# Attention scores of a unit issued as one run of products over five accumulator banks, instead of three runs

## The chip, the cores and the metric

The kernel runs on one core of a Trainium2 chip. The metric is the device time of one execution in microseconds (us). Below, TensorE is the matrix engine (PE in the profile, its weight loads PEld), VectorE is DVE, ScalarE is ACT, GpSimd is POOL, and SyncE (SP) issues the DMAs.

## The reference

Windowed attention with a linear distance bias on 8 batches of 8 heads, then a two-layer MLP with GELU on the attention's output:

```
batch, n_heads, seq, head_dim = 8, 8, 576, 64        # window 128
scores = q @ k.T / sqrt(64)
scores = where(0 <= i - j < 128, scores - slope[h] * |i - j|, -1e9)
attn = exp(scores - max); attn = attn / (sum(attn) + 1e-9)
x = (attn @ v) as (8 * 576, 512)
out = gelu(x @ w_in) @ w_out                          # 512 -> 2048 -> 512
```

The inputs are float32. The kernel splits each operand into a high and a low float16 part and adds three products (high by high, low by high, high by low); only the first batch's attention and the first token tile's second layer run on float32 operands.

## The kernel before, in words

**Units.** Attention works in units of one batch `b` and one pair of heads `hp`, so 4 units to a batch, 32 in all. A query block of 64 rows sees a window of 192 keys. The 18 blocks of a unit (9 blocks, 2 heads) are held two and two on the 128 partitions, as 9 groups of 128 x 192 scores (`GROUPS`, L43). Groups are put into PSUM in five banks of two or one groups: `BANKS = ((0, 1), (2, 3), (4,), (5, 6), (7, 8))`. Banks (0,1) and (5,6) belong to head 0, banks (2,3) and (7,8) to head 1, and bank (4,) holds block 8 of both heads. The first three banks are called EVEN, the last two ODD.

**Scores.** `scores(st, banks)` takes the PSUM banks of a piece, issues its products (L394), has VectorE bring each bank to SBUF as `s`, scaled and with the bias added (L416), and GpSimd write the masked corner (L421). Every product is a 64 x 64 weight (a query block) with 192 keys streaming. The head sets which half of the array's rows it uses, the half of the group which half of its columns. In a piece of two banks four products in a row use the four quarters of the array; in the piece of bank (4,) two in a row do. A unit has three pieces (`PIECES`): banks (0,1) and (2,3) with 24 products, bank (4,) with 6, banks (5,6) and (7,8) with 24.

**Softmax and weighing.** `softmax` does EVEN and then ODD: VectorE takes the row maximum (L480), ScalarE the exponentials with their sums (L483, 5 and 4 of them, given to the planner with a raised priority), VectorE the reciprocals (L486, L487), GpSimd the high half of the weights (`e_main`, L489), VectorE the low half (L491, under the helper's line L143), and one transposing DMA on the SP queue writes `et` (L492). `weigh` multiplies `et` with v (`av`, L529) in two PSUM banks, one for each of the token tiles that a batch's rows fall into (`b` and `b + 1`, since a batch has 576 rows and a tile 512). ScalarE (L542) and VectorE (L543, shown as L143) bring each `av` into the MLP's input `x` of that tile. `x` has two buffers.

**The MLP.** Tokens go in 9 tiles `t` of 512. A tile has 32 steps. In steps 0 to 15 `mlp_in` makes one block of the hidden layer with 12 products of 128 x 512 (`h`, L573), ScalarE applies Gelu (L589), GpSimd and VectorE split it into the halves `g` (L590, L591 shown as L143). In steps 16 to 31 `mlp_out` adds 12 products to an output bank `o` (L611), four steps to a bank.

**Banks.** PSUM has 8 banks, in two tags of 4: "att" for scores (from batch 1 on) and for `av`, "mm" for `h` and `o`.

**Order.** Into tile `t`'s 32 steps the work of batch `b = t + 1` is set by hand (L720 to L757). For `t >= 2`, `SCORES_AT = (2, 11, 16, 21)` and `WEIGH_AT = (12, 20, 25, 30)`: the three pieces of unit 0 follow steps 2, 3 and 4, and after the third comes its softmax; unit 0 is weighed after step 12; and so on. Step 1 splits v and issues the loads of the next batch, step 6 takes the next v's maximum, step 24 splits the next q and k. The program text is the order of priority, and a planner (`TileContext` with `schedule_with_timeline_sim=True`) turns it into a fixed order of instructions on each engine: where an instruction's operand or buffer isn't free by the planner's own reckoning, a later one that is ready goes ahead of it. On the chip, each engine then keeps to that order and waits on semaphores.

The order by hand, in the lines that matter:

```
for t in range(1, NTILE):
    b = t + 1
    ...
    for step in range(2 * NFC):
        ...mlp_in(t, step) or 12 products of mlp_out...
        if step in at:
            hp, i = at[step]
            scores(unit(b, hp), BANKS[PIECES[i]])
            if i == 2:
                softmax(unit(b, hp))
        ...
        if step in weigh_at:
            weigh(unit(b, weigh_at.index(step)))
```

Of the kernel before, what the change touches and what calls it, by code (L numbers as in the profile page):

```python
# [11 lines left out]
F32 = mybir.dt.float32  # L12
I32 = mybir.dt.int32
AF = mybir.ActivationFunctionType
ALU = mybir.AluOpType
AX = mybir.AxisListType

B, H, S, D = 8, 8, 576, 64
WINDOW = 128
P = 128  # L20
QB = 64
# [8 lines left out]
W = 3 * QB  # L30
PAD = W - QB
NKB = 5
NEG = -1.0e30
# [3 lines left out]
EXACT = 1  # L37
# [5 lines left out]
GROUPS = [(h, j) for h in range(2) for j in (0, 4)] + [(None, 8)] + [(h, j) for h in range(2) for j in (1, 5)]  # L43
NG = len(GROUPS)
NEVEN = 5
FIRST_MM = (2,)
EXP_AHEAD = 400
BANKS = ((0, 1), (2, 3), (4,), (5, 6), (7, 8))
PIECES = (slice(0, 2), slice(2, 3), slice(3, 5))


@with_exitstack
def attention_gelu_mlp(
# [10 lines left out]
    nc = tc.nc  # L64
    pool = ctx.enter_context(tc.tile_pool(name="sb", bufs=1))
    psum = ctx.enter_context(tc.tile_pool(name="ps", bufs=1, space=bass.MemoryType.PSUM))

    def small(shape, name, bufs, tag=None, dt=F32):
        return pool.tile(shape, dt, tag=tag or name, name=name, bufs=bufs)
# [8 lines left out]
    ident, upper, never = (adders[:, n] for n in range(3))  # L78
# [206 lines left out]
    qbuf = pool.tile([P, 2, NPAIR * S], F16, name="qbuf")  # L285
    kbuf = pool.tile([P, 2, KS], F16, name="kbuf")
    qbuf32 = qbuf.rearrange("p h s -> p (h s)").bitcast(F32)
    kbuf32 = kbuf.rearrange("p h s -> p (h s)").bitcast(F32)
# [4 lines left out]
    v32s, qk32, csq = {}, {}, {}  # L293

    def load_v(b):
        v32 = pool.tile([P, NPAIR, NKB, P], F32, tag="v32", name=f"v32_{b}", bufs=1)
        for hp in range(NPAIR):
            nc.sync.dma_start(v32[:, hp], vp[b, hp].rearrange("(n p) d -> p n d", p=P))
        v32s[b] = v32
# [18 lines left out]
    def split_v(b):  # L318
        v32 = v32s.pop(b).rearrange("p h n d -> p (h n d)")
        hi = vbuf[:, 0].rearrange("p h n d -> p (h n d)")  # L320
        lo = vbuf[:, 1].rearrange("p h n d -> p (h n d)")
        nc.scalar.activation(hi, v32, AF.Copy, scale=scv[b])  # L322
        low_part(lo, v32, scv[b], hi)
# [38 lines left out]
    def bias_of(hp, head):  # L362
        return bias_p[:, hp : hp + 1, :] if head is None else bias_h[:, 2 * hp + head : 2 * hp + head + 1, :]

    def scores(st, banks):

        b, hp, u = st.b, st.hp, st.u
        if not hasattr(st, "s"):
            st.ps = {}
            st.s = pool.tile([P, NG, W], F32, tag="s", name=f"s{u}", bufs=2)  # L370
        s = st.s
        exact = b < EXACT
        terms = (None,) if exact else ((0, 0), (1, 0), (0, 1))

        def operands(term, r, j):
            q, k = slice(hp * S + j * QB, hp * S + (j + 1) * QB), slice(hp * S + PAD + (j - 2) * QB, hp * S + PAD + (j + 1) * QB)
            if exact:
                return qbuf32[r, q], kbuf32[r, k]
            return qbuf[r, term[0], q], kbuf[r, term[1], k]

        ps = st.ps
        for bank in banks:
            tag = "mm" if b == 0 and bank[0] in FIRST_MM else "att"
            ps[bank] = psum.tile([P, 2, 256], F32, tag=tag, name=f"sc{u}_{bank[0]}", bufs=4)
        for n in range(len(banks[0])):
            for i, term in enumerate(terms):
                for half in range(2):
                    for bank in banks:
                        head, j = GROUPS[bank[n]]
                        h = half if head is None else head  # L390
                        jj = j if head is None else j + 2 * half
                        r, o = slice(h * D, h * D + D), slice(half * D, half * D + D)
                        a, m = operands(term, r, jj)
                        nc.tensor.matmul(  # L394
                            ps[bank][o, n, 0:W], a, m, start=(i == 0), stop=(i == len(terms) - 1 and b > 0),
                            skip_group_check=True,
                        )
            if b == 0:
                for bank in banks:
                    adds = [(slice(0, W), ident, bias_of(hp, GROUPS[bank[n]][0])[:, 0])]  # L400
                    gap = (2 - GROUPS[bank[n]][1]) * QB
                    if gap > 0:

                        adds.append((slice(0, gap), upper, never[:, 0:gap]))
                    for i, (c, a, m) in enumerate(adds):
                        nc.tensor.matmul(
                            ps[bank][:, n, c], a, m, start=False, stop=(i == len(adds) - 1), skip_group_check=True
                        )
        if b == 0:
            return  # L410
        cs = csq[b]
        for bank in banks:
            head, k = GROUPS[bank[0]][0], len(bank)
            j = GROUPS[bank[0]][1]
            bias = bias_of(hp, head)
            nc.vector.scalar_tensor_tensor(  # L416
                out=s[:, bank[0] : bank[0] + k, :], in0=ps[bank][:, 0:k, 0:W], scalar=cs,
                in1=bias.broadcast_to([P, k, W]) if k > 1 else bias, op0=ALU.mult, op1=ALU.add,
            )
            if j < 2:  # L420
                nc.gpsimd.memset(s[0:D, bank[0], 0 : (2 - j) * QB], NEG)  # L421

    EVEN, ODD = slice(0, NEVEN), slice(NEVEN, NG)

# [124 lines left out]
    def tile_scales(t, ns):  # L549


        k = len(ns)
        r = slice(ns[0], ns[-1] + 1)
        big = k > 1
        gs = small([P, k], f"gs{t}_{ns[0]}", 2, tag=f"gs{int(big)}")
        nc.vector.tensor_scalar(gs, pww[:, r], pwx[t], 2.0 ** -26, op0=ALU.mult, op1=ALU.mult)
        if t == 0:
            for n in ns:
                gsc[t, n] = gs[:, n - ns[0] : n - ns[0] + 1]
            return  # L560
        sg = small([P, k], f"sg{t}_{ns[0]}", 2, tag=f"sg{int(big)}")
        nc.vector.tensor_scalar(sg, sww[:, r], sx[t], 2.0 ** -22, op0=ALU.mult, op1=ALU.mult)
        for n in ns:
            gsc[t, n], gsg[t, n] = gs[:, n - ns[0] : n - ns[0] + 1], sg[:, n - ns[0] : n - ns[0] + 1]
# [30 lines left out]
    def out_scale(t):  # L595
        so[t] = small([P, 1], f"so{t}", 2, tag="so")
        nc.vector.tensor_scalar(so[t], pwm, pwx[t], 2.0 ** -17, op0=ALU.mult, op1=ALU.mult)
# [29 lines left out]
    def unit(b, hp):  # L627
        if (b, hp) not in units:
            units[b, hp] = Unit(b, hp)
        return units[b, hp]  # L630

    def all_scores(st):
        for piece in PIECES:
            scores(st, BANKS[piece])

    fetched = iter(range(2 * NWP))

# [16 lines left out]
    fetch(NWP)  # L654

    all_scores(unit(0, 0))
    softmax_first(unit(0, 0))
    all_scores(unit(0, 1))
# [43 lines left out]
    scores_at, weigh_at, split_at = {1: 2, 3: 3}, {2: 0, 4: 1, 6: 2}, {5: 0, 6: 2, 7: 4}  # L702
# [18 lines left out]
    for t in range(1, NTILE):  # L721
        b = t + 1
        scores_at, weigh_at = (SCORES_AT, WEIGH_AT) if t > 1 else ((8, 14, 18, 22), (17, 22, 26, 30))
        at = {s + i: (hp, i) for hp, s in enumerate(scores_at) for i in range(3)}
        tile_scales(t, range(NWP))
        out_scale(t)
        for step in range(2 * NFC):
            if step < NFC:
                mlp_in(t, step)
            else:  # L730
                tb, q = divmod(step - NFC, 4)
                for fc in range(4 * q, 4 * q + 4):
                    mlp_out(t, tb, fc)
            if b >= B:
                continue
            if step in at:
                hp, i = at[step]
                scores(unit(b, hp), BANKS[PIECES[i]])
                if i == 2:
                    softmax(unit(b, hp))  # L740
            if step == 1:
                split_v(b)
                if b + 1 < B:
                    load_v(b + 1)
                    load_qk(b + 1)
            if step == 6:
                if b + 1 < B:
                    stat_v(b + 1)
                else:

                    pwx[B], sx[B] = pwv[B - 1], scv[B - 1]
                    cx_last = small([P, 1], "cxl", 1)
                    nc.vector.tensor_scalar(cx_last, pwv[B - 1], sx[B], 2.0 ** -27, op0=ALU.mult, op1=ALU.mult)
            if step in weigh_at:
                weigh(unit(b, weigh_at.index(step)))
            if step == SCORES_AT[-1] + 3 and b + 1 < B:
                split_qk(b + 1)  # L757
# [36 lines left out]
```

## Time and profile before

| What | Value |
|---|---|
| Median of 3 runs | 963.53 us (963.16 to 969.68) |
| The profiled execution's own time | 963.32 us |
| Its span, first to last instruction | 961.4 us |
| TensorE busy | 922.8 us, 96% |
| VectorE busy | 643.7 us, 67% |
| ScalarE busy | 436.6 us, 45% |
| GpSimd busy | 255.8 us, 27% |

The profile is of one execution. A row of the timeline gives the start, the length, the engine, the line, and how many instructions of one kind it holds; the length of a row of products goes to the modelled end of the last one, so the time that a run takes is read from its start to the start of the next row. A value in square brackets at the end of a row is idle time of the engine ahead of it and what ended it. A row of the waits tells who waited for whom: us in total, times, longest. Tile 2 begins at 297 us, tile 7 at 792 us; tiles 2 to 6 are those in which batches 3 to 7 are worked on.

### The profile page before, as it was taken

Reading aid. Unit: us, or ns where it says so; the run is one execution under the profiler, and the core shown is the slowest. Engines: PE = TensorE matmul, PEld = TensorE weight load, DVE = VectorE, ACT = ScalarE, POOL = GpSimd, SP = SyncE. Lnnn points to the kernel's source line nnn. Section 1 sums busy time; section 2 is a strip of 40 time slices with the busy share of each in tenths; the row PEclk is TensorE's granted clock in tenths of the full one; section 3 lists DMA queues with packets and bytes.
Section 4 is the critical chain, followed back from the end, with each engine's and each line's share of the span. In section 5 each row is a group of like instructions: output and inputs, shape, how many; then the busy total and the mean of one; then the engine's idle time right before and its main releaser. Section 6 shows DMA issues by size and latency. Waiting matters only on the chain. (4 is left out here: it accounts for less than half of the span.)

```text
span 961.4 us, 17491 instructions
## 1 busy us (share of the span) xinstructions
PE 922.8 (96%) x6996; PEld 446.1 (46%) x6996; DVE 643.7 (67%) x1270; ACT 436.6 (45%) x943; POOL 255.8 (27%) x516
## 2 busy tenths in 40 slices
PE   7988999769999899999999999999999999999998
PEld 3553444334454345444544444444544454444443
DVE  6699999989985877688767876777566632201300
ACT  6565445545553565256526653564465413201200
POOL 1010103324441433144313530363144312201200
PEclk9789999989999999999999999999999999999999
DMA  9525742972466224713372357244313430000000
GB/s 320 201 69 167 235 137 39 217 201 60 84 130 157 50 50 80 206 40 61 85 194 49 59 94 171 56 78 83 79 25 57 83 73 12 1 22 23 1 12 33
DMA packets 172451, 91.18 MB, mean 95 GB/s; under 512 B 132561, under 2 KB 153169, under 8 KB 172241
## 3 DMA queue, kind: packets, MB, share of 16 engines
q1 hardware_dynamic: 172368, 90.06, 37.9%
q8 instruction: 55, 0.90, 0.4%
q14 instruction: 28, 0.22, 0.1%
HBM read 46.53 MB, written 9.44 MB: 58 GB/s over the span
## 5 line engine op out<-in xcount | busy, mean ns | idle before, releaser
L573 PE MATMUL h<-x,wi 128*128 128x512 f16 x1728 | 386.7, 382 | 9.6 <-ACT g L589 3.9
L573 PEld LDWEIGHTS <-wi 128*128 128x128 f16 x1728 | 166.6, 98 | 212.4 <-issue 14.0
L611 PE MATMUL o<-wo,g 128*128 128x512 f16 x1152 | 259.9, 379 | 0.0
L611 PEld LDWEIGHTS <-g 128*128 128x128 f16 x1536 | 145.9, 98 | 174.3
L590 POOL TENSOR_SCALAR g<-g,sg 128x512 f16<-128x512 f32 x128 | 100.1, 786 | 288.7 <-ACT g L589 281.7
L143 DVE SCALAR_TENSOR_TENSOR g<-g,sg,g 128x512 f16<-128x512 f32 x128 | 106.2, 843 | 92.0 <-POOL g L590 92.0
L483 ACT ACTIVATE s<-s,nmax 128x192 f32<-128x192 f32 x252 | 111.2, 443 | 107.7 <-DVE nmax L480 105.0
L489 POOL TENSOR_SCALAR e_main<-s,z 128x192 f16<-128x192 f32 x252 | 124.3, 511 | 114.9 <-issue 37.3
L589 ACT ACTIVATE g<-h,gs 128x512 f32<-128x512 f32 x128 | 85.9, 687 | 137.3 <-PE h L573 108.5
L143 DVE SCALAR_TENSOR_TENSOR e_main<-s,z,e_main 128x192 f16<-128x192 f32 x252 | 112.1, 487 | 11.1 <-POOL e_main L489 10.8
L611 PE MATMUL o<-wo_first,g 128*128 128x512 f16 x384 | 88.2, 379 | 0.0
L394 PE MATMUL sc<-kbuf,qbuf 64*64 64x192 f16 (+1 forms) x1656 | 77.6, 266 | 9.4 <-DMA kbuf<-kp 4.4
L416 DVE SCALAR_TENSOR_TENSOR s<-sc,cs,bias_h 128x384 f32<-128x384 f32 x112 | 63.9, 606 | 15.1 <-PE sc L394 14.9
L542 ACT ACTIVATE x<-av,cx 128x448 f16<-128x448 f32 (+6 forms) x52 | 23.9, 477 | 86.0 <-PE av L529 85.8
L480 DVE TENSOR_REDUCE nmax<-s 128x5 f32<-128x960 f32 (+1 forms) x56 | 58.5, 1044 | 2.2
L608 PE MATMUL o<-zo,g 128*128 128x512 f32 x128 | 57.0, 598 | 0.0
L529 PE MATMUL av<-et,vbuf 128*64 128x128 f16 (+1 forms) x1680 | 45.2, 213 | 11.4 <-DMA et<-e_main 10.3
L421 POOL MEMSET s<- 64x128 f32 (+1 forms) x112 | 19.6, 176 | 134.5 <-DVE s L416 133.7
L619 ACT ACTIVATE ob<-o,so 128x512 f32<-128x512 f32 x16 | 10.9, 679 | 96.9 <-PE o L611 96.8
L394 PEld LDWEIGHTS <-qbuf 64*64 64x64 f16 x1512 | 35.2, 106 | 42.0 <-issue 39.4
L529 PEld LDWEIGHTS <-vbuf 128*64 128x64 f16 x1680 | 42.2, 113 | 21.3 <-issue 19.5
L621 DVE TENSOR_SCALAR ob<-o,so 128x512 f32<-128x512 f32 x16 | 11.9, 744 | 60.0 <-PE o L611 60.0
(128 smaller groups left out, 715.1 us busy)
## 6 DMA issues: line engine op xcount, KB each, us to landing
v<-vp SPq DMA_DIRECT2D x32, 320.0 KB, 5.0
out<-ob SPq DMA_DIRECT2D x36, 256.0 KB, 2.1
raw<-w_in SPq DMA_DIRECT2D x8, 1024.0 KB, 14.1
raw<-w_out SPq DMA_DIRECT2D x8, 1024.0 KB, 5.0
q<-qp SPq DMA_DIRECT2D x7, 1152.0 KB, 6.1
k<-kp SPq DMA_DIRECT2D x7, 1152.0 KB, 6.3
qbuf<-qp SPq DMA_DIRECT2D x4, 288.0 KB, 4.5
kbuf<-kp SPq DMA_DIRECT2D x4, 288.0 KB, 4.9
```

The lines of the kernel that those rows point to most:

```text
L143: nc.vector.scalar_tensor_tensor(out=dst, in0=src, scalar=scale, in1=high, op0=ALU.mult, op1=ALU.subtract)
L394: nc.tensor.matmul(ps[bank][o, n, 0:W], a, m, start=(i == 0), stop=(i == len(terms) - 1 and b > 0), skip_group_check=True,)
L416: nc.vector.scalar_tensor_tensor(out=s[:, bank[0] : bank[0] + k, :], in0=ps[bank][:, 0:k, 0:W], scalar=cs, in1=bias.broadcast_to([P, k, W] ...
L480: nc.vector.tensor_reduce(out=nmax[:, r], in_=s[:, r], axis=AX.X, op=ALU.max, negate=True)
L483: nc.scalar.activation(s[:, i, :], s[:, i, :], AF.Exp, bias=nmax[:, i : i + 1], accum_out=z[:, i : i + 1])
L489: nc.gpsimd.tensor_scalar(e[:, i, 0, c], s[:, i], z[:, i : i + 1], 1.0, op0=ALU.mult, op1=ALU.mult)
L529: nc.tensor.matmul(av[r, (j - blocks[0]) * QB : (j - blocks[0] + len(js)) * QB], v32s[b][:, hp, kb, r] if b < EXACT else vbuf[:, vi, hp, k ...
L573: nc.tensor.matmul(ph, wi[n][:, a, cc, k * P : (k + 1) * P], x[:, cc, b, :], start=(i == 0), stop=(i == 3 * NCC - 1),)
L589: nc.scalar.activation(g32, ph, AF.Gelu, scale=gsc[t, n])
L590: nc.gpsimd.tensor_scalar(g[:, r, 0], g32, gsg[t, n], 1.0, op0=ALU.mult, op1=ALU.mult)
L608: nc.tensor.matmul(o, g[:, r, c], zo[n][:, n % 2, k * DM : (k + 1) * DM], start=(fc == 0), stop=(fc == NFC - 1))
L611: nc.tensor.matmul(o, g[:, r, a, c], wo[n][:, b, k, :], start=(fc == 0 and i == 0), stop=(fc == NFC - 1 and i == 2),)
```

## The change

From tile 2 on, that is for batches 3 to 7 (20 units), a unit's scores are no longer three pieces after three steps. All 54 products are issued together after the third of these steps (4, 13, 18, 23), in the order banks (0,1) and (2,3), banks (5,6) and (7,8), bank (4,); then come the five copies to `s`, in the order of the banks, and the softmax. Five banks are taken at once: four of tag "att" and, for bank (4,), one of tag "mm". The units of batches 1 and 2 keep their three pieces, those of batch 0 have a function of their own, `scores_first`, with the same instructions as before.

```diff
+TOGETHER = (BANKS[0:2], BANKS[3:5], BANKS[2:3])
...
-    def scores(st, banks):
+    def scores(st, pieces):
...
+        for bank in sum(pieces, ()):
+
+            tag = "mm" if len(bank) == 1 and len(pieces) > 1 else "att"
+            ps[bank] = psum.tile([P, 2, 256], F32, tag=tag, name=f"sc{u}_{bank[0]}", bufs=4)
+        terms = ((0, 0), (1, 0), (0, 1))
+        for banks in pieces:
+            for n in range(len(banks[0])):
+                for i, (a, m) in enumerate(terms):
+                    for half in range(2):
+                        for bank in banks:
...
+                            nc.tensor.matmul(
+                                ps[bank][o, n, 0:W], qbuf[r, a, q : q + QB], kbuf[r, m, k : k + W],
+                                start=(i == 0), stop=(i == len(terms) - 1), skip_group_check=True,
+                            )
+        for bank in sorted(ps):
...
+            nc.vector.scalar_tensor_tensor(
+                out=s[:, bank[0] : bank[0] + k, :], in0=ps[bank][:, 0:k, 0:W], scalar=csq[b],
...
     def all_scores(st):
         for piece in PIECES:
-            scores(st, BANKS[piece])
+            if st.b < EXACT:
+                scores_first(st, BANKS[piece])
+            else:
+                scores(st, (BANKS[piece],))
...
-        at = {s + i: (hp, i) for hp, s in enumerate(scores_at) for i in range(3)}
+        whole = t >= 2
+        at = {s + i: (hp, i) for hp, s in enumerate(scores_at) for i in ((2,) if whole else range(3))}
...
-                scores(unit(b, hp), BANKS[PIECES[i]])
+                scores(unit(b, hp), TOGETHER if whole else (BANKS[PIECES[i]],))
```

More of the change, by code (lines that the diff above doesn't have):

```diff
@@ L363, in bias_of, with scores_first @@
         return bias_p[:, hp : hp + 1, :] if head is None else bias_h[:, 2 * hp + head : 2 * hp + head + 1, :]
-    def scores(st, banks):
+    def scores(st, pieces):
+        b, hp, u = st.b, st.hp, st.u
+        if not hasattr(st, "s"):
+            st.s = pool.tile([P, NG, W], F32, tag="s", name=f"s{u}", bufs=2)
+        s = st.s
+        ps = {}
+        for bank in sum(pieces, ()):
[7 more added lines that the diff above has]
+                        for bank in banks:
+                            head, j = GROUPS[bank[n]]
+                            h, j = (half, j) if head is None else (head, j + 2 * half)
+                            r, o = slice(h * D, h * D + D), slice(half * D, half * D + D)
+                            q = hp * S + j * QB
+                            k = q + PAD - 2 * QB
+                            nc.tensor.matmul(
[3 more added lines that the diff above has]
+        for bank in sorted(ps):
+            head, j = GROUPS[bank[0]]
+            k = len(bank)
+            near = bias_of(hp, head)
+            nc.vector.scalar_tensor_tensor(
+                out=s[:, bank[0] : bank[0] + k, :], in0=ps[bank][:, 0:k, 0:W], scalar=csq[b],
+                in1=near.broadcast_to([P, k, W]) if k > 1 else near, op0=ALU.mult, op1=ALU.add,
+            )
+            if j < 2:
+                nc.gpsimd.memset(s[0:D, bank[0], 0 : (2 - j) * QB], NEG)
+    def scores_first(st, banks):
         b, hp, u = st.b, st.hp, st.u
@@ L370, in scores, with operands @@
             st.s = pool.tile([P, NG, W], F32, tag="s", name=f"s{u}", bufs=2)
[L371 to L375, printed above, removed]
+        def operands(r, j):
             q, k = slice(hp * S + j * QB, hp * S + (j + 1) * QB), slice(hp * S + PAD + (j - 2) * QB, hp * S + PAD + (j + 1) * QB)
-            if exact:
-                return qbuf32[r, q], kbuf32[r, k]
-            return qbuf[r, term[0], q], kbuf[r, term[1], k]
+            return qbuf32[r, q], kbuf32[r, k]
@@ L381, in scores @@
         ps = st.ps
         for bank in banks:
-            tag = "mm" if b == 0 and bank[0] in FIRST_MM else "att"
+            tag = "mm" if bank[0] in FIRST_MM else "att"
             ps[bank] = psum.tile([P, 2, 256], F32, tag=tag, name=f"sc{u}_{bank[0]}", bufs=4)
         for n in range(len(banks[0])):
[L386 to L397, printed above, removed]
@@ L398, in scores @@
-            if b == 0:
-                for bank in banks:
[L400 to L421, printed above, removed]
+            for half in range(2):
+                for bank in banks:
+                    head, j = GROUPS[bank[n]]
+                    h = half if head is None else head
+                    jj = j if head is None else j + 2 * half
+                    r, o = slice(h * D, h * D + D), slice(half * D, half * D + D)
+                    a, m = operands(r, jj)
+                    nc.tensor.matmul(ps[bank][o, n, 0:W], a, m, start=True, stop=False, skip_group_check=True)
@@ new lines, in scores_first @@
+            for bank in banks:
+                adds = [(slice(0, W), ident, bias_of(hp, GROUPS[bank[n]][0])[:, 0])]
+                gap = (2 - GROUPS[bank[n]][1]) * QB
+                if gap > 0:
+                    adds.append((slice(0, gap), upper, never[:, 0:gap]))
+                for i, (c, a, m) in enumerate(adds):
+                    nc.tensor.matmul(
+                        ps[bank][:, n, c], a, m, start=False, stop=(i == len(adds) - 1), skip_group_check=True
+                    )
```

## The prediction

> **What bounds the kernel now.** I read the page's busy shares first, then the busy times by tile, then TensorE's timeline through a tile, and last the waits.
>
> ```profile
> span 961.4 us, 17491 instructions
> ...
> PE 922.8 (96%) x6996; PEld 446.1 (46%) x6996; DVE 643.7 (67%) x1270; ACT 436.6 (45%) x943; POOL 255.8 (27%) x516
> ```
>
> ```profile
> core 0: us, PE busy (x) PEld busy (x) DVE busy (x) ACT busy (x) POOL busy (x), PEclk, DMA share, GB/s
> 297.00:399.00 102.00, 98.86 (x912) 47.90 (x910) 74.30 (x152) 51.33 (x112) 32.71 (x68) 0.98 0.41 94
> 399.00:497.00 98.00, 97.93 (x821) 47.41 (x820) 74.94 (x151) 51.63 (x112) 32.56 (x68) 1.00 0.43 98
> 497.00:596.00 99.00, 96.68 (x863) 46.72 (x862) 74.03 (x150) 50.99 (x112) 32.30 (x68) 1.00 0.45 97
> 596.00:695.00 99.00, 97.82 (x820) 47.20 (x819) 70.33 (x150) 53.73 (x113) 33.38 (x68) 1.00 0.34 73
> 695.00:792.00 97.00, 97.00 (x842) 46.97 (x841) 57.56 (x111) 45.50 (x109) 32.65 (x68) 1.00 0.34 61
> ```
>
> These are tiles 2 to 6, the only ones the change touches. TensorE is busy in all but 0 to 3 us of each, at nearly full granted clock; VectorE, the next busiest, has a quarter of the tile free. So time is gained here only by shorter work on TensorE, and lost by new waits of TensorE.
>
> The timeline of TensorE in tile 4 shows what the scores cost it:
>
> ```profile
> 531.41 2.76 PE L573 MATMUL h<-x,wi 128*128 128x512 f16 x12
> 534.11 0.43 PE L394 MATMUL sc<-kbuf,qbuf 64*64 64x192 f16 x6
> 534.47 1.60 PE L529 MATMUL av<-et,vbuf 128*64 128x128 f16 x66
> 536.00 2.76 PE L573 MATMUL h<-x,wi 128*128 128x512 f16 x12
> ...
> 544.50 2.75 PE L611 MATMUL o<-wo_first,g 128*128 128x512 f16 x12
> 547.19 0.69 PE L394 MATMUL sc<-kbuf,qbuf 64*64 64x192 f16 x24
> 547.81 2.76 PE L611 MATMUL o<-wo,g 128*128 128x512 f16 x12
> 550.50 0.43 PE L394 MATMUL sc<-kbuf,qbuf 64*64 64x192 f16 x6
> 550.87 2.76 PE L611 MATMUL o<-wo,g 128*128 128x512 f16 x12
> 553.56 0.69 PE L394 MATMUL sc<-kbuf,qbuf 64*64 64x192 f16 x24
> 554.18 2.76 PE L611 MATMUL o<-wo,g 128*128 128x512 f16 x12
> 556.78 2.75 PE L611 MATMUL o<-wo_first,g 128*128 128x512 f16 x12
> 559.47 1.60 PE L529 MATMUL av<-et,vbuf 128*64 128x128 f16 x66
> 561.00 2.76 PE L611 MATMUL o<-wo,g 128*128 128x512 f16 x12
> ```
>
> Two groups of 12 with nothing between them start 556.78 - 554.18 = 2.60 us apart. What stands between two groups costs their distance less 2.60. A piece of 24 products: 547.81 - 544.50 - 2.60 = 0.71 us. The piece of 6: 550.87 - 547.81 - 2.60 = 0.46. An `av` run alone: 561.00 - 556.78 - 2.60 = 1.62. The 6 together with `av` (step 12 of unit 1): 536.00 - 531.41 - 2.60 = 1.99, so there the 6 add only 0.37, because the change of shape into and out of small products is paid once for both.
>
> **What a longer run costs.** Four products in a row use four quarters of the array, so 24 are 6 rounds; the 6 of bank (4,) go two and two, 3 rounds. From 0.71 and 0.46, three rounds cost 0.25, a round 0.083, and the fixed part is 0.21 us a run. The whole unit is 6 + 6 + 3 = 15 rounds: 0.21 + 15 x 0.083 = 1.46 us. The trace has one such run, in the first tile, where the planner put several pieces together:
>
> ```profile
> 144.41 1.43 PE L394 MATMUL sc<-kbuf,qbuf 64*64 64x192 f16 x42
> 145.77 3.70 PE L608 MATMUL o<-zo,g 128*128 128x512 f32 x8
> ```
>
> Its 42 products take 1.36 us to the next start; beside it, the 24 take 547.81 - 547.19 = 0.62. If the cost went by the number of products (0.25 us for 18), the 42 would take 0.87. By rounds, 15 of them take 0.62 + 9 x 0.083 = 1.37. Rounds it is, and a run of three pieces isn't stretched by its length.
>
> [...]
>
> **The change part by part.**
>
> *Three runs become one, units 0, 2 and 3.* Before: 0.71 + 0.46 + 0.71 = 1.88. After: 1.46. Gain 0.42 us a unit, all of it on TensorE's path.
>
> *Unit 1.* Its 6 shared their entry with `av`, so before it cost 0.71 + 0.37 + 0.71 = 1.79; in one run it would gain 0.33. But the run needs all four "att" banks, and at step 13 one of them isn't free. `weigh` of unit 0, just ahead at step 12, fills two, and the second belongs to tile t + 2, whose `x` buffer is still being read by `mlp_in` of tile t up to step 15 (544.50):
>
> ```profile
> 535.06 0.42 ACT L542 ACTIVATE x<-av,cx 128x192 f16<-128x192 f32 x1 [0.16 <-PE av L529]
> ...
> 542.88 1.28 ACT L483 ACT_TABLE_LOAD   x1
> 545.81 0.45 ACT L483 ACTIVATE s<-s,nmax 128x192 f32<-128x192 f32 x1 [1.64 <-DVE nmax L480]
> ...
> 547.57 0.56 ACT L542 ACTIVATE x<-av,cx 128x384 f16<-128x384 f32 x1
> ```
>
> ```profile
> 529.67 4.27 DVE L143 SCALAR_TENSOR_TENSOR g<-g,sg,g 128x512 f16<-128x512 f32 x4
> 533.86 1.13 DVE L416 SCALAR_TENSOR_TENSOR s<-sc,cs,bias_h 128x384 f32<-128x384 f32 x2
> ...
> 535.57 0.41 DVE L416 SCALAR_TENSOR_TENSOR s<-sc,cs,bias_p 128x192 f32<-128x192 f32 x1
> ...
> 542.11 1.13 DVE L416 SCALAR_TENSOR_TENSOR s<-sc,cs,bias_h 128x384 f32<-128x384 f32 x2
> ...
> 548.17 0.62 DVE L143 SCALAR_TENSOR_TENSOR x<-av,cx,x 128x384 f16<-128x384 f32 x1
> ```
>
> The first `av` bank leaves at once, the second at 548.79, 12 us later. Before, three free banks were enough for any piece. After, bank (7,8) must wait, and the planner will let what is ready go ahead: 24 + 12 + 6 products at step 13 (the 12 on one head are two in a round, so 15 rounds, 1.46 us), the other 12 after step 15 or 16 (6 rounds, 0.71). Unit 1 then costs 2.17 instead of 1.79, a loss of 0.38. Its bounds are the gain of 0.33 (if the planner finds four banks free) and, from above, the late second half in the rivals. I take the loss, because the read of `x` up to step 15 lies in the program and not in anyone's speed.
>
> *The five copies to `s`.* 2 x 1.13 + 0.41 = 2.67 us of VectorE at a stretch, where they came in three parts. They delay the rows behind them on VectorE (`g`, the maximum of v at step 6) by up to 2 us. Cover: `g` of the first half isn't read before step 16, and the next taker of "att" banks is two or more steps (5.2 us) away, but for unit 1. Counted 0; if the cover goes, see the third rival.
>
> *The "mm" bank.* At worst VectorE starts 2.5 us late (531.41 to 533.86, behind four `g` rows) and reaches bank (4,) in its place, so the bank is back some 5 us after the run, two groups of `h`; three banks hold three groups. Counted 0.
>
> *Softmax later.* EVEN's scores come two steps later, but EVEN waited for bank (4,) anyway, and ODD's chain ends last. With both maxima ready together, ScalarE can do nine exponentials in one block (9 x 0.45) instead of two blocks with a Gelu between. That ends unit 0's chain earlier; I count nothing for it in the sum.
>
> *Waits that are there now.* By tile, TensorE's waits in tiles 2 to 6, and last one from before them:
>
> ```profile
> PE h L573 <- ACT g L589: 2.7, 2, 2.4
> PE av L529 <- DMA et<-e_main: 0.5, 1, 0.5
> ```
>
> ```profile
> PE av L529 <- DMA et<-e_main: 1.7, 1, 1.7
> PE h L573 <- ACT g L589: 0.6, 1, 0.6
> ```
>
> ```profile
> PE av L529 <- DVE g L143: 1.2, 1, 1.2
> ```
>
> ```profile
> PE sc L394 <- DVE s L416: 3.4, 1, 3.4
> ```
>
> The first five add up to 6.7 us (tiles 2, 4 and 5). They lie on the softmax chain and on Gelu, which the change rearranges: between all of it gone (-6.7) and as much again (+6.7). I take 0. The last is a scores run that stood waiting for the copy of an earlier one: it is what a too tight hold on the banks costs.
>
> **Sum.** A tile: 3 x 0.42 - 0.38 = 0.88 us; five tiles: 4.4. Against the profiled execution's 963.32 us (span 961.4 and 1.9 around it; the median is 963.53), that is **958.9 us**.
>
> **Rivals.**
>
> *Nothing breaks.* Unit 1 finds its banks and all 20 runs are whole: 15 x 0.42 + 5 x 0.33 = 7.95, so 955.4. For it: the planner may weigh unit 0 after unit 1's scores. Against it: `weigh` is ahead in the program. If the waits of 6.7 us shrink by half or more as well, both cases reach 955 to 950. Nine exponentials in one block speak for this.
>
> *Unit 1's second half comes too late (slower).* Before, its last copy ends at 543.24 (542.11 + 1.13), and its last transposing DMA lands as these rows tell:
>
> ```profile
> 543.96 9.79 SPq L492 DMA_TRANSPOSE et<-e_main  x2
> ```
>
> ```profile
> DMA to landing us min/median/max: 4.6/4.6/4.6
> ```
>
> The second was issued in 551 to 552, so it lands at about 556.3, and `av` starts at 559.47: 3.1 us to spare. After, if the bank leaves at 548.79 as now, 12 products (0.71) and a copy (0.57) end at 550.1, 6.8 us later than before; 3.7 us of wait a tile, 18.5 in five: 977.4. It decides from 0.9 us of wait a tile on. Against the full price: the bank's copy at 547.57 stands behind four exponentials of ODD that will no longer be ahead of it, and a planner that sees `et` late puts `av` one group (2.60) further back; then some 1 us is left, and 964.
>
> *Evacuation becomes the bound.* [...] In rows: the run takes 1.46 and its copies 2.67; with VectorE behind and ScalarE in its 6.6 us block (9 x 0.45 and two table loads of 1.28), the ten units of the first half could each hold an `h` by 1 us: 958.9 + 10 = 969. Against it: one such wait of 2.4 is the longest now, with shorter blocks but more table loads.
>
> *The change doesn't do what it says.* The planner cuts most runs as in tile 0, and entries stay as many as before: 963.
>
> **Chances.** Forecast 0.45; nothing breaks or the waits shrink 0.27; second half too late 0.15 (a third of it near the full price); evacuation 0.05; no real change 0.08. The range that leaves out 2 in 10 runs from 950 to 970. A measurement of this kernel tells about 1% (9.6 us) from no change. Faster by more, below 953.9, needs whole runs and shrunken waits together: 0.13. Slower by more, above 973, needs the late half near its full price: 0.09. Within: 0.78.
>
> **What would show it.** Right: in tiles 2 to 6 the rows of L394 lose their x24, x6, x24 pattern; units 0, 2, 3 show one row of 54 with about 1.46 between the groups around it; unit 1 shows 42 and then 12 after step 15, with the 12 right behind the copy of `x`. Wrong: a row of 54 for unit 1, or 54 taking more than 1.6 us; waits of `av` on `et` at step 20 of every tile; waits of `h` on Gelu after steps 4 and 13; clock below 0.98 in these tiles. The forecast falls if waits of TensorE in tiles 2 to 6 sum to over 12 us or under 2.

## The result and the profile after

| | Before | After |
|---|---|---|
| Median, us (20 runs each) | 962.78 (953.61 to 969.68) | 971.39 (963.53 to 977.84) |
| Ratio, 95% interval | | 1.0102 [1.0075, 1.0129] |
| Profiled execution, us (span) | 963.32 (961.4) | 971.82 (970.0) |

The kernel became 1.0% slower; 958.9 had been predicted. Ratios leave out runs over 1.5% above the fastest of their kernel (mean granted clock 0.960 to 0.975 where it is on record, 0.966 to 0.995 in those kept), so a ratio can rest on fewer runs than the median beside it. The page of the changed kernel, its head:

```profile
span 970.0 us, 17465 instructions
...
PE 923.4 (95%) x6996; PEld 455.0 (47%) x6996; DVE 646.4 (67%) x1270; ACT 412.0 (42%) x925; POOL 258.1 (27%) x516
```

TensorE has the same 6996 products. ScalarE has 18 instructions and 24.6 us less: it loads its tables 42 times in place of 60 (18 x 1.28 = 23.0 us), since nine exponentials now mostly stand in one block. By tile, in the columns of the prediction's second fence:

```profile
398.00:499.00 101.00, 97.95 (x830) 48.65 (x828) 74.71 (x150) 45.88 (x107) 33.56 (x68) 0.98 0.40 93
499.00:600.00 101.00, 97.92 (x856) 49.44 (x854) 74.53 (x150) 46.09 (x108) 33.24 (x68) 0.98 0.42 96
600.00:703.00 103.00, 99.44 (x884) 50.18 (x882) 70.05 (x150) 47.76 (x109) 33.78 (x68) 0.98 0.35 75
```

Tiles 3 to 5 (97.3, 99.5 and 98.3 us long before, from the first `h` of one to that of the next) are 101.0, 100.6 and 103.0 us long, at a granted clock of 0.98 in place of 1.00. TensorE's timeline shows where, here the whole of tile 4 up to unit 2 and the same place of the other four tiles (in square brackets is the idle time ahead of the row, and what ended it):

```profile
337.64 2.77 PE L544 MATMUL av<-et,vbuf 128*64 128x128 f16 x66 [2.75 <-DMA et<-e_main]
...
438.42 1.81 PE L544 MATMUL av<-et,vbuf 128*64 128x128 f16 x54 [2.73 <-DMA et<-e_main]
440.16 4.13 PE L588 MATMUL h<-x,wi 128*128 128x512 f16 x12
...
499.06 1.67 PE L588 MATMUL h<-x,wi 128*128 128x512 f16 x7
500.89 1.55 PE L544 MATMUL av<-et,vbuf 128*64 128x128 f16 x54 [0.16 <-DMA et<-e_main]
...
513.92 1.43 PE L388 MATMUL sc<-kbuf,qbuf 64*64 64x192 f16 x54
515.29 21.17 PE L588 MATMUL h<-x,wi 128*128 128x512 f16 x96
539.25 2.77 PE L544 MATMUL av<-et,vbuf 128*64 128x128 f16 x66 [2.80 <-DMA et<-e_main]
541.96 2.76 PE L588 MATMUL h<-x,wi 128*128 128x512 f16 x12
544.65 1.42 PE L388 MATMUL sc<-kbuf,qbuf 64*64 64x192 f16 x42
546.00 3.41 PE L588 MATMUL h<-x,wi 128*128 128x512 f16 x15
549.35 0.68 PE L388 MATMUL sc<-kbuf,qbuf 64*64 64x192 f16 x12
549.96 2.12 PE L588 MATMUL h<-x,wi 128*128 128x512 f16 x9
...
554.50 5.34 PE L626 MATMUL o<-wo,g 128*128 128x512 f16 x24
559.78 1.43 PE L388 MATMUL sc<-kbuf,qbuf 64*64 64x192 f16 x54
561.14 2.76 PE L626 MATMUL o<-wo,g 128*128 128x512 f16 x12
...
640.25 2.20 PE L544 MATMUL av<-et,vbuf 128*64 128x128 f16 x54 [2.77 <-DMA et<-e_main]
...
739.44 1.57 PE L544 MATMUL av<-et,vbuf 128*64 128x64 f16 x60 [1.48 <-DMA et<-e_main]
```

The scores cost what was forecast: a whole run 561.14 - 554.50 - 2 x 2.60 = 1.44 us, unit 1's 42 products 546.00 - 541.96 - 2.60 = 1.44. What is new is the wait at step 12: the `av` run of **unit 0** waits for its `et` in every tile, 2.75, 2.73, 2.80, 2.77 and 1.48 us. From the end of each of the four long waits, give or take 1.1 us, the granted clock is 0.50 for 3.4 us (which waits had this with them is in the last section). The windows around the wait in tile 4:

```profile
538.00:540.00 2.00, 0.75 (x22) 0.75 (x24) 0.70 (x1) 0.00 (x0) 0.16 (x1) 0.63 0.34 63
540.00:542.00 2.00, 2.00 (x53) 1.94 (x50) 1.08 (x2) 0.42 (x1) 0.00 (x0) 0.51 0.00 0
```

The clock column, the last but two, reads 0.51 from 540 to 542. The `av` run then takes 541.96 - 539.25 = 2.71 us, 1.18 more than the 1.53 of before (536.00 - 534.47); in tile 3 the 12 `h` behind it take 4.13 in place of 2.76.

**The account.** From the first `h` of tile 2 to the first of tile 7, before took 495.9 us and after 502.9: 7.0 of the 8.5 us between the two profiled executions. The other 1.5 lie ahead of tile 2, where both issue the same products, in the same order but for two neighbours. Between the starts of two successive products there is a usual distance for each kind of pair (two of 128 x 512: 2.60 / 12 = 0.217 us); what goes beyond it by over 0.3 us adds up to 7.2 us in these tiles before and 14.5 after. With the scores' gain worked out by the same distances (4.5 us), a rest of 7.0 + 4.5 - 7.3 = 4.2 us is left. I put it down to the half clock, in four places where before had one. A second trace bears this out: the kernel with the maximum of v at step 9 (below) waits 13.0 us where the change waits 14.0, its profiled execution has a mean granted clock of 0.980 where the change's has 0.976, and its tiles 2 to 6 are 497.4 us long, 5.6 less.

**Why unit 0's `et` is late.** VectorE in tile 4 of after, from the maximum of v on:

```profile
514.14 2.82 DVE L209 TENSOR_REDUCE stv<-v 128x1 f32<-128x2560 f32 x1 [1.90 <-DMA v<-vp]
...
517.60 1.12 DVE L396 SCALAR_TENSOR_TENSOR s<-sc,cs,bias_h 128x384 f32<-128x384 f32 x2
...
520.00 1.14 DVE L396 SCALAR_TENSOR_TENSOR s<-sc,cs,bias_h 128x384 f32<-128x384 f32 x2
521.06 0.41 DVE L396 SCALAR_TENSOR_TENSOR s<-sc,cs,bias_p 128x192 f32<-128x192 f32 x1
521.45 1.99 DVE L495 TENSOR_REDUCE nmax<-s 128x4 f32<-128x768 f32 x2
...
531.74 2.58 DVE L144 SCALAR_TENSOR_TENSOR e_main<-s,z,e_main 128x192 f16<-128x192 f32 x5
```

and the same work in tile 4 of before:

```profile
505.52 1.14 DVE L416 SCALAR_TENSOR_TENSOR s<-sc,cs,bias_h 128x384 f32<-128x384 f32 x2 [0.49 <-PE sc L394]
508.22 2.82 DVE L208 TENSOR_REDUCE stv<-v 128x1 f32<-128x2560 f32 x1 [1.56 <-DMA v<-vp]
...
511.62 0.41 DVE L416 SCALAR_TENSOR_TENSOR s<-sc,cs,bias_p 128x192 f32<-128x192 f32 x1
...
527.77 1.78 DVE L143 SCALAR_TENSOR_TENSOR e_main<-s,z,e_main 128x192 f16<-128x192 f32 x3
```

Before, EVEN's two big copies were over before v's maximum came, and EVEN's five exponentials were done before ODD's four began. After, the maximum of v is taken right as the run of 54 starts, so the run's first copy comes 3.7 us behind that start (517.60 - 513.92), and bank (4,), which EVEN needs, is copied last of the five. GpSimd in after:

```profile
525.55 2.27 POOL L504 TENSOR_SCALAR e_main<-s,z 128x192 f16<-128x192 f32 x4 [3.53 <-issue]
...
530.00 3.35 POOL L504 TENSOR_SCALAR e_main<-s,z 128x192 f16<-128x192 f32 x5
```

The four groups of ODD go through first, EVEN's five last. VectorE's last row ends at 534.32, 35.26 us into a tile that starts at 499.06; before, its last ended at 529.55, 32.63 us into a tile that starts at 496.92. The transposing DMA of the last half follows, here before (issued at 529.58, four groups) and after (issued at 534.34, five groups):

```profile
DMA to landing us min/median/max: 4.2/4.2/4.2
DMA to landing us min/median/max: 4.9/4.9/4.9
```

To the hundredth, it lands 4.27 us behind VectorE before (533.82) and 4.89 in after (539.21). `av` stood at 37.55 us into the tile before (534.47), so the chain had 37.55 - 32.63 - 4.27 = 0.65 us to spare; in tile 3 it had 0.41 and in tile 5 0.13. In after, `av`'s place is at 37.40 (536.46, where the eight groups of `h` end). So the chain is 2.63 later, its DMA 0.62 longer and the place 0.15 earlier: less the 0.65, this is 2.75 us. The row has 2.80; `av` starts 0.04 us behind the landing.

### The profile page after: what moved, and what is told of

It reads as the page before. It is cut to its first block, busy times and chain, and to the rows that moved or that the text cites. A ratio compares the mean times of both kernels' runs of the same rounds, so it can differ in the third digit from the quotient of the medians.

```text
span 970.0 us, 17465 instructions
## 1 busy us (share of the span) xinstructions
PE 923.4 (95%) x6996; PEld 455.0 (47%) x6996; DVE 646.4 (67%) x1270; ACT 412.0 (42%) x925; POOL 258.1 (27%) x516
## 4 chain that ended last, share of the span: by engine, by line
PE 53%; DVE 26%; DMA 12%; issue 3%; ACT 3%; SPq 2%; POOL 1%; DVEq 0%; POOLq 0%; ACTq 0%
PE o L626 26%; PE h L588 19%; DMA et<-e_main 6%; PE av L544 4%; DVE e_main L144 4%; PE sc L388 3%; DVE s L396 3%; DMA q<-qp 2%; DMA v<-vp 2%; DVE nmax L495 2%; DVE g L144 2%; DVE stq L209 2%; DVE stv L209 1%; DVE kbuf L144 1%; DVE vbuf L144 1%
## 5 line engine op out<-in xcount | busy, mean ns | idle before, releaser
L626 PE MATMUL o<-wo,g 128*128 128x512 f16 x1152 | 256.7, 379 | 0.0
L605 POOL TENSOR_SCALAR g<-g,sg 128x512 f16<-128x512 f32 x128 | 97.8, 770 | 306.3 <-ACT g L604 303.6
L504 POOL TENSOR_SCALAR e_main<-s,z 128x192 f16<-128x192 f32 x252 | 128.1, 528 | 134.3 <-ACT x L557 51.8
L544 PE MATMUL av<-et,vbuf 128*64 128x128 f16 (+1 forms) x1680 | 48.4, 220 | 22.8 <-DMA et<-e_main 22.7
L544 PEld LDWEIGHTS <-vbuf 128*64 128x64 f16 x1680 | 45.6, 118 | 34.5 <-issue 23.1
L388 PE MATMUL sc<-kbuf,qbuf 64*64 64x192 f16 x1512 | 49.6, 246 | 4.0 <-DVE s L396 4.0
L388 PEld LDWEIGHTS <-qbuf 64*64 64x64 f16 x1512 | 38.2, 107 | 28.5 <-issue 28.4
L636 DVE TENSOR_SCALAR ob<-o,so 128x512 f32<-128x512 f32 x16 | 11.9, 745 | 57.3 <-PE o L626 57.3
```

Of the source, the lines that this page charges most:

```text
L388: nc.tensor.matmul(ps[bank][o, n, 0:W], qbuf[r, a, q : q + QB], kbuf[r, m, k : k + W], start=(i == 0), stop=(i == len(terms) - 1), skip_gr ...
L504: nc.gpsimd.tensor_scalar(e[:, i, 0, c], s[:, i], z[:, i : i + 1], 1.0, op0=ALU.mult, op1=ALU.mult)
L544: nc.tensor.matmul(av[r, (j - blocks[0]) * QB : (j - blocks[0] + len(js)) * QB], v32s[b][:, hp, kb, r] if b < EXACT else vbuf[:, vi, hp, k ...
L605: nc.gpsimd.tensor_scalar(g[:, r, 0], g32, gsg[t, n], 1.0, op0=ALU.mult, op1=ALU.mult)
L626: nc.tensor.matmul(o, g[:, r, a, c], wo[n][:, b, k, :], start=(fc == 0 and i == 0), stop=(fc == NFC - 1 and i == 2),)
```

## The experiments

The first theory (A): unit 0's chain, as just told, costs the time; of its parts, A1 is that the chain starts only at step 4, A2 the order of the banks and A3 the maximum of v. Its rival (B): the loss comes from unit 1's cut run and what follows from it. All ratios are to the kernel before.

**Give the chain two steps more.**

```
-    SCORES_AT, WEIGH_AT = (2, 11, 16, 21), (12, 20, 25, 30)
+    SCORES_AT, WEIGH_AT = (2, 11, 16, 21), (14, 20, 25, 30)
```

> The changed kernel with unit 0 weighed after step 14 instead of 12 in tiles 2 to 6. Theory A (unit 0's softmax ends too late for its weighing at step 12, TensorE stands 1.5 to 2.8 us a tile, and a wait of 2.7 us also halves the granted clock for some 3 us): two more groups of h (5.2 us) cover it, no wait of av at unit 0 over 0.5 us, no clock of 0.5; the 12.5 us of waits and some 6 us of slow clock go, and unit 1's run finds four free banks and is whole (5 x 0.7 us): 948 to 955. Theory B (the loss is in the cut run of unit 1 and what follows from it): unit 1's run is whole here too, so B also expects a gain, but only the 5 x 0.7 us: some 967.

Measured 955.2 us, 0.9951 [0.9926, 0.9976], where B expected some 967. The wait of unit 0's `av` is gone, and as this `av` no longer holds a bank at step 13, unit 1's run is whole in all five tiles (18 of the 20 runs are; two of unit 0 are sent off in two parts, 7 + 47 and 2 + 52):

```profile
534.27 1.60 PE L544 MATMUL av<-et,vbuf 128*64 128x128 f16 x66
...
554.44 1.60 PE L544 MATMUL av<-et,vbuf 128*64 128x128 f16 x66 [1.46 <-DVE ob L636]
```

The first row is unit 0 (no bracket), the second unit 1 at step 20, which now waits some 1.4 to 1.5 us in tiles 3 to 6. The bracket names a copy of VectorE, but `et` landed at 554.30, just ahead of `av`: it is the same fault one unit later, since unit 1's run is whole as well. The control, the same edit in the kernel before:

> The kernel before, three pieces as they were, with unit 0 weighed after step 14 instead of 12 in tiles 2 to 6: what the later weighing does without the change. Its waits at step 12 (1.1 us in one tile) are all that it can win: 958 to 963. If whole runs are worth some 1.6 us a tile (four units at 0.42 and 0.33), the changed kernel with the same weighing (955.2) must be 5 to 8 us under this. If this run comes to 955 as well, the gain there was the later weighing's and whole runs win nothing.

961.28 us, 1.0015 [0.999, 1.0041]. The later place gains nothing by itself in the timed runs; with it the whole runs are worth about 6 us.

**Unit 0 in three pieces, units 1 to 3 whole.**

```
-        at = {s + i: (hp, i) for hp, s in enumerate(scores_at) for i in ((2,) if whole else range(3))}
+        at = {s + i: (hp, i) for hp, s in enumerate(scores_at) for i in ((2,) if whole and hp else range(3))}
...
-                scores(unit(b, hp), TOGETHER if whole else (BANKS[PIECES[i]],))
+                scores(unit(b, hp), TOGETHER if whole and hp else (BANKS[PIECES[i]],))
```

> The changed kernel, but unit 0 of each batch keeps its three pieces at steps 2, 3, 4; units 1 to 3 are whole runs. Theory A: the waits at step 12 fall back to those of the kernel before (0 to 1.2 us) and the clock stays: 958 to 962, a little under the kernel before, as units 2 and 3 gain 0.42 us each and unit 1 loses 0.38 a tile. Theory B: unit 1's run stays cut, so the time stays near 970.

968.31 us, 1.0110 [1.0068, 1.0153]: the loss stays, as B expected, and A as I had it missed. The waits at step 12 shrank, but 9.0 us of waits on Gelu came. The waits of TensorE in tiles 2 to 6, and VectorE in tile 4 (which starts at 497.7):

```profile
PE h L588 <- ACT g L604: 9.0, 5, 2.4
PE av L544 <- DMA et<-e_main: 3.7, 6, 1.2
```

```profile
513.98 2.82 DVE L209 TENSOR_REDUCE stv<-v 128x1 f32<-128x2560 f32 x1 [2.23 <-DMA v<-vp]
516.72 0.41 DVE L396 SCALAR_TENSOR_TENSOR s<-sc,cs,bias_p 128x192 f32<-128x192 f32 x1
```

The maximum of v is late here too, 16.3 us into the tile where before has it at 11.3, and bank (4,)'s copy stands behind it; ScalarE's exponentials wait for that, and its Gelus stand behind them. So what delays the maximum isn't in unit 0. Before shows the same pattern in its tile 2, the one tile where its own maximum is late (16.5 us into the tile): there stand its 2.4 us of wait on Gelu.

**Only unit 0 whole** (`whole and not hp` in both places).

> The change for unit 0 alone; units 1 to 3 keep three pieces at three steps. Theory A (the loss is unit 0's late chain): waits of av at step 12 stay in most tiles; the first piece of unit 1 at step 11 and the second at step 12 stand ahead of av and take 1.1 us of the 2.8, so 1.2 to 1.8 us a tile and little slow clock: 961 to 968. Theory B (the cut run of unit 1): unit 1 is in pieces as before, so no loss at all: 959 to 962 and no waits over 1 us at step 12.

962.84 us, 1.002 [0.9994, 1.0045]: within the range for A and less than 1 us above that for B. The waits at step 12 are 2.00, 0.37, 0.34, 1.47 and 0.39 us by tile, so they stay long in two tiles only, where A expected most. The maximum of v is back at 11.1 to 11.9 us in tiles 3 to 5. This led to theory C: unit 3's whole run at step 23 makes its own `et` later, so the planner puts its `av` behind the tile's end (500.89 in after, 1.8 us into tile 4, where before has it 2.1 ahead, at 494.78). These rows of before show it:

```profile
494.78 1.55 PE L529 MATMUL av<-et,vbuf 128*64 128x128 f16 x54
...
496.92 7.93 PE L573 MATMUL h<-x,wi 128*128 128x512 f16 x36
```

The split of v comes after that `av`, the load of the next v after the split, and its maximum after the load: from unit 3's `av` to the maximum it is 13.4 to 13.5 us in tiles 3 to 5 of before and 13.2 to 13.4 in those of after. In tile 2, where the unit 3 ahead of it is in pieces in both kernels, the maximum is late in both (16.5 us into the tile before, 15.9 after), so the wait of 2.75 in tile 2 of after isn't unit 3's doing.

**Unit 3 in pieces, 0 to 2 whole** (`whole and hp < 3`).

> The changed kernel, but unit 3 of each batch keeps its three pieces; units 0 to 2 are whole runs. Theory C (unit 3's whole run makes its weighing some 4 us later, past the end of the tile; the split of v, the load of the next v and the maximum of v follow it, and that maximum then lands right ahead of unit 0's copies): unit 3 is weighed 2 to 4 us ahead of the tile's first h again (in the changed kernel 2 us behind it), the maximum of v starts 11 to 12 us into tiles 3 to 5 instead of 15, waits at step 12 of these tiles fall from 2.8 to under 1.6 us and no clock of 0.5 follows them: 956 to 963. If unit 0's own run makes the chain late, whatever v does: the waits stay at 2.4 to 2.9 us, 967 to 972.

966.87 us, 1.0097 [1.0064, 1.0130]. The mechanism of C is there, tile 4 (from 498.6) once more:

```profile
509.93 2.82 DVE L209 TENSOR_REDUCE stv<-v 128x1 f32<-128x2560 f32 x1 [3.18 <-DMA v<-vp]
```

```profile
536.43 1.60 PE L544 MATMUL av<-et,vbuf 128*64 128x128 f16 x66 [1.43 <-DMA et<-e_main]
537.96 2.76 PE L588 MATMUL h<-x,wi 128*128 128x512 f16 x12
```

The maximum is 11.3 us into the tile, the wait 1.43 in place of 2.80, and the `av` run takes its normal 1.53. What is left of the wait isn't v's. VectorE's last row ends only 0.23 us later in the tile than before (32.86), but EVEN's DMA is again 0.62 longer, and `av`'s place is 1.19 earlier (36.36 for 37.55), because unit 1's first two pieces no longer stand ahead of it. Yet the expected time, 956 to 963, missed, and the ratio doesn't differ from the change's. In microseconds the median is 4.5 below the change's 971.39, but before's median beside it was lower as well, 958.08 for 962.78.

**EVEN's banks copied first.**

```
-TOGETHER = (BANKS[0:2], BANKS[3:5], BANKS[2:3])
+TOGETHER = (BANKS[0:2], BANKS[2:3], BANKS[3:5])
```

> The changed kernel with bank (4,) in its old place, between the two pairs, in the one run, so that EVEN is complete first. Theory A1 (the chain is late because all of it starts at step 4, behind the maximum of v on VectorE): waits at step 12 stay at 2 us or more, 967 to 972. Theory A2 (it is late because EVEN, with five groups, is now the half that ends the chain): the tail gets one group shorter and overlaps ODD's exponentials, waits at step 12 fall below 1.5 us and the slow clock goes: 957 to 963.

961.49 us, 0.9987 [0.9951, 1.0024], 1.1% under the change. The waits at step 12 are 2.10, 0.87, 1.43, 0.69 and 0 us by tile; here tile 4's, after which the run of 66 takes 1.60 (the granted clock is 1.00 from 533 to 539):

```profile
534.58 1.60 PE L544 MATMUL av<-et,vbuf 128*64 128x128 f16 x66 [1.43 <-DMA et<-e_main]
```

The order of two pieces in one tuple, with the same products and copies, is worth the whole loss; A2 holds. Unit 1's run is still cut into 42 and 12 in all five tiles, so B is out. The edit reorders all 20 units, though, and v's maximum is still late, 14.4 to 16.4 us into the tile.

**The maximum of v at step 9, in the program** (`if step == (9 if whole else 6):`).

> The changed kernel with the maximum of the next v taken at step 9 instead of 6 in tiles 2 to 6. If that 2.8 us row on VectorE, now ahead of unit 0's copies, is what makes its chain late (theory A3), waits at step 12 fall below 0.5 us and the slow clock goes: 952 to 960. If the order of the banks is (A2), the chain is late without it too: waits of 1.5 us or more stay, over 965.

969.25 us, 1.0088 [1.0047, 1.0129], the waits 2.75, 2.36, 2.79, 2.77 and 1.47, nearly as without the edit. The planner left the row where it was, when v lands (14.4 to 15.5 us into the tile), so this told nothing of A3.

**The next v held back until unit 0's copies are made** (a column of its buffer is first written from unit 0's `s`, so the load waits for it).

```
-    def load_v(b):
+    def load_v(b, gate=None):
...
+        if gate is not None:
+            for hp in range(NPAIR):
+                nc.vector.tensor_copy(v32[:, hp, 0, 0:1], gate)
...
-                    load_v(b + 1)
+                    if not whole:
+                        load_v(b + 1)
...
+            if step == 4 and whole and b + 1 < B:
+                load_v(b + 1, unit(b, 0).s[:, 1, W - 1 : W])
```

> The changed kernel with the load of the next v held back (a one-column copy from unit 0's s into its buffer first, 4 small rows a tile), so that the planner now puts the maximum of v behind unit 0's copies and maxima on VectorE; moving only the step did not move that row. Tile 6 of the changed kernel has no next v, and its wait at step 12 is 1.5 us without slow clock, against 2.8 with it in tiles 2 to 5. Theory A3 (the maximum of v ahead of the copies makes the first 1.3 us and so the slow clock): waits of 1.0 to 1.6 us in tiles 2 to 5, no clock of 0.5 behind them: 957 to 963. If the row only moves to where VectorE is needed for the low halves of the weights, waits stay at 2.5 to 3 us: 968 to 972.

979.57 us, 1.0206 [1.0161, 1.025], above both expected ranges. The waits at step 12 fell to 1.36, 1.48, 2.35, 1.40 and 1.48 us, in four tiles to about the 1.48 of after's tile 6, where there is no next v: so A3 is worth some 1.3 us of wait a tile. But the scale that `x` is multiplied with comes from v's maximum too, so the banks that hold `av` leave later, and unit 1's run at step 13 stands waiting for them, in the waits of tiles 2 to 6:

```profile
PE sc L391 <- DVE x L144: 10.6, 4, 3.9
```

**Whole runs at the step of the first piece** (2, 11, 16, 21, not 4, 13, 18, 23).

```
-        at = {s + i: (hp, i) for hp, s in enumerate(scores_at) for i in ((2,) if whole else range(3))}
+        at = {s + (0 if whole else i): (hp, i) for hp, s in enumerate(scores_at) for i in ((2,) if whole else range(3))}
```

> The whole runs come after the first of the three steps (2, 11, 16, 21) instead of the last. Theory A: unit 0's chain starts two steps (5.2 us) earlier, ahead of the maximum of v at step 6, so the waits of 1.5 to 2.8 us at step 12 are gone; unit 1's run at step 11 comes before unit 0 is weighed, so it is whole: 950 to 956. A rival: the order of the banks and the burst of five copies make the chain late, wherever it begins; then waits of over 1 us at step 12 stay, and the time is above 962.

983.68 us, 1.0243 [1.0198, 1.0287]; 950 to 956 was expected. The waits at step 12 are gone but for 1.5 us in tile 2. In their place unit 2's run at step 16 stands half done for a bank, in every tile:

```profile
554.71 0.76 PE L388 MATMUL sc<-kbuf,qbuf 64*64 64x192 f16 x25
559.41 0.93 PE L388 MATMUL sc<-kbuf,qbuf 64*64 64x192 f16 x29 [3.94 <-DVE x L144]
```

Here the prediction's held bank is at work at full price: 3.8 to 4.0 us a tile. Behind the wait in tile 4 the granted clock reads 0.75 from 559 to 562 and 0.68 from 562 to 565.

**Both remedies together:** EVEN's banks first and `WEIGH_AT = (14, 21, 25, 30)`.

> The changed kernel with bank (4,) back in the middle of the run, unit 0 weighed after step 14 and unit 1 after step 21 (before 12 and 20). Both causes of waits found so far are gone: no wait of av over 0.5 us in tiles 2 to 6, no slow clock, 20 whole runs: 946 to 951, ratio to before 0.985 to 0.990. If waits of unit 1 only move on by a step, 953 to 956.

Median of six runs 954.26 us; the ratio, 0.9843 [0.9795, 0.9890], rests on three of them. So it was run again, and once more with the held-back v:

> The same kernel as the one with bank (4,) in the middle and weighing after 14 and 21, once more, because its six runs lay between 942.7 and 959.4: 943 to 956, ratio to before 0.982 to 0.992.

> Both: bank (4,) in the middle, weighing after 14 and 21, and the load of the next v held back. With et 3.8 us or more ahead of its weighing already, the row of VectorE is covered and nothing is left to win there: the same as without holding v back, within 3 us; slower by up to 5 us if the late v delays the weighing's scale factors.

949.31 us, 0.9892 [0.9844, 0.9939], and 948.82 us, 0.9857 [0.9801, 0.9914]: no difference between the two. The first one's waits of TensorE in tiles 2 to 6:

```profile
PE av L544 <- DMA et<-e_main: 1.5, 2, 1.2
PE h L588 <- ACT g L604: 1.1, 3, 0.5
```

With or without v held back, this version beats both kernels: before by 1.1 to 1.4%, the change (1.0102) by 2% or more. The pieces of before were not run with unit 1 weighed at 21, so what that later place would give without whole runs isn't shown.

Waits of TensorE in tiles 2 to 6 (of one profiled execution) beside the ratios:

| Kernel | Waits, us | Ratio |
|---|---|---|
| both remedies, v held back | 1.3 | 0.9857 |
| both remedies, again | 2.6 | 0.9892 |
| unit 0 weighed at 14 | 7.9 | 0.9951 |
| only unit 0 whole | 8.4 | 1.002 |
| EVEN's banks first | 9.6 | 0.9987 |
| unit 3 in pieces | 11.0 | 1.0097 |
| maximum of v at step 9 | 13.0 | 1.0088 |
| unit 0 in pieces | 13.3 | 1.0110 |
| the change | 14.0 | 1.0102 |
| v held back | 19.2 | 1.0206 |
| at the first step | 23.6 | 1.0243 |

A straight line through the eleven (ratios times 962) gives 1.75 us for each us waited, the half clock being part of it. Unit 3 in pieces lies 5 us above that line. The control doesn't fit it either: its profiled execution waits 3.0 us where before waits 6.7, and its profiled tiles 2 to 6 are 3.6 us shorter (492.3), but its timed runs aren't. Both stay open.

## Why the prediction was wrong, step by step

- **Three runs become one, and unit 1.** Right. Whole runs cost 1.44 us (1.46 forecast); in tiles 2 and 3 unit 0's was sent off in two parts (7 + 47 and 2 + 52). Unit 1 was cut as forecast, its two parts cost 1.44 + (549.96 - 546.00 - 15 x 2.60 / 12) = 2.15 (2.17), and the scores of tiles 2 to 6 gained 4.5 us (4.4). In unit 1, 42 products take 546.00 - 544.65 = 1.35 us and in unit 0 54 take 515.29 - 513.92 = 1.37: both are 15 rounds, so here the rounds decide. One detail failed: the last 12 ran at 549.35, before the copy of `x` that holds the bank, so they had another bank.
- **The five copies to `s`: counted 0.** The cover I named was for the rows behind the copies. The row ahead of them, v's maximum (2.82 us), I took to be where it was; it had moved 4 us later and on top of the copies, and that costs about 1.3 us of wait a tile.
- **"EVEN's scores come two steps later, but EVEN waited for bank (4,) anyway … That ends unit 0's chain earlier".** This is the step that failed. Before, EVEN's two big copies were done before ODD's products had run, and its maximum (513.47) before ODD's banks were copied (514.60); the exponentials came in two blocks, but the first block's groups went through GpSimd while the second was worked out. After, nothing of the unit starts before the run, and bank (4,) as the last of five made EVEN, the longer half, the last. In tile 4 the chain ended 2.6 us later, and its DMA, now of five groups, took 0.6 longer. I had counted a block of exponentials and not the distance from the chain's end to `av`, which the trace of before gives: 0.13 to 0.65 us to spare in tiles 3 to 5. Nor had I seen that unit 1's first two pieces, which stood ahead of that `av`, would now stand behind it.
- **"Waits that are there now … I take 0".** They went from 6.7 to 14.0 us, and by the prediction's own test (over 12) the forecast falls. The half clock, which I had looked for only as a sign, added some 4 us, the rest of the account above. It came with all four long waits of after, but with v's maximum at step 9 the 66 products behind a wait of 2.79 us took their usual time (last section).
- **The "mm" bank: counted 0.** Right as to `h`: the waits of `h` on Gelu fell from 3.3 to 0.3 us. What the tuple's order does to the copies had not been weighed.
- **Rivals.** *Unit 1's second half too late* had the right mechanism, a chain that lands late for its `av`, at the wrong unit: in after no `av` at step 20 waits. *Nothing breaks* (955.4) is what weighing unit 0 at step 14 gave, 955.2, with unit 1 whole; its waits were 7.9 us, so the near agreement is partly chance. *Evacuation* didn't show. None of the rivals named unit 0, nor what unit 3's later `av` does to the next tile.

What the experiments show: unit 0's chain is the loss (two steps more, or EVEN's banks first, take it away). Unit 0's whole run alone doesn't make it (1.002), and with unit 0 in pieces but v's maximum late the waits only move to Gelu (1.0110). In tiles 3 to 5 unit 3's whole run is what makes v's maximum late (it is early again with unit 3 in pieces, or with unit 0 alone whole). What stays open is how much unit 3 in pieces gains: its profiled tiles 2 to 6 are 5.8 us shorter than the change's (497.2) and its median is 4.5 us lower, but its ratio is the same.

## What to carry to other kernels

When pieces of work are joined, look at what the first piece's followers had been doing while the later pieces ran, and work out the slack of each chain at its consumer: here 0.13 to 0.65 us of slack decided over a gain of 4.5. Joining also moves everything that is behind it into the next stage; follow the last unit of a stage over the boundary. The consumer's place should be moved with the producer's: whole runs with the old weighing steps lost 1.0%, with unit 0 weighed two steps and unit 1 one step later and the right order of banks they gained 1.1 to 1.4%.

## What the runs showed of the hardware

Where the granted clock isn't full in tiles 2 to 6 of after, it is 0.50, in four stretches of 3.4 us that begin at 337.1, 439.5, 538.5 and 640.9. Before has one such stretch, from 329.8 to 333.2. Each begins within 1.2 us of the end of a wait of TensorE: 2.75, 2.73, 2.80 and 2.77 us in after, and in before 2.43 us, on Gelu, which ends at 328.76. After's wait of 1.48 us in tile 6 has none.

The length of the wait alone doesn't tell them apart. With v's maximum at step 9, the 66 products behind a wait of 2.79 us took their usual time:

```profile
537.29 1.60 PE L544 MATMUL av<-et,vbuf 128*64 128x128 f16 x66 [2.79 <-DMA et<-e_main]
```

Behind the shorter wait of 2.35 us in the kernel with v held back, the same 66 products took 2.71, near the 2.77 of after's tiles 2 and 4:

```profile
544.18 2.71 PE L547 MATMUL av<-et,vbuf 128*64 128x128 f16 x66 [2.35 <-DMA et<-e_main]
```

Before's wait of 1.7 us ends at 594.06, and the clock of the 4 us from there is 1.00:

```profile
594.00:598.00 4.00, 3.94 (x78) 2.63 (x79) 1.23 (x3) 3.08 (x3) 0.00 (x0) 1.00 0.02 5
```

What else decides whether the half clock comes with a wait isn't shown.

The times of one kernel spread with the mean granted clock: among the 20 runs of after, 977.84 us at 0.970 and 963.53 at 0.987, with a correlation of -0.81. One stretch of 3.4 us at 0.50 lowers the mean over 970 us by 3.4 x 0.50 / 970 = 0.0018, so these two runs would lie some nine stretches apart, by this estimate. Whether it is such stretches that differ between timed runs isn't shown, as only one execution of each kernel was profiled.
